# Attention beside a gated MLP on one core: a reordered opening, transposed sums for the last softmax reciprocals, and retuned scheduling constants

## The chip, the cores and the metric

The kernel runs on one core of one Trainium2 chip. The metric is the device time of one execution in microseconds, as the median of several runs. All runs compared here are fast (within 1.5% of the fastest run of the same kernel). The granted clock is the share of full speed that TensorE's clock had, as the profile gives it. Inside a trace, times count from the start of the span; the span is some 2 us shorter than the device time.

## The reference

```python
B, S, D, H, F = 1, 2048, 512, 32, 1792            # Dh = 16
def _A_ref(x, wqkv, wo):
    qkv = (x @ wqkv).reshape(B, S, 3, H, Dh).transpose(2, 0, 3, 1, 4)
    q, k, v = qkv[0], qkv[1], qkv[2]
    p = softmax(einsum("bhqd,bhkd->bhqk", q, k) * Dh ** -0.5)
    o = einsum("bhqk,bhkd->bhqd", p, v)
    return o.transpose(0, 2, 1, 3).reshape(B, S, D) @ wo
def _B_ref(x, W_gate, W_up, W_down):
    gate = x @ W_gate
    return (gate * (gate > 0) * (x @ W_up)) @ W_down
xn = _layernorm(A_x)                               # eps 1e-5
return A_x + _A_ref(xn, A_wqkv, A_wo) + _B_ref(xn, B_W_gate, B_W_up, B_W_down)
```

Softmax over 32 heads of 2048 x 2048 scores is 134 million exponentials. That is the load that everything else is arranged around.

## The kernel before

The program does not write its instructions in order. It describes each as an operation with an engine, a modelled duration, what it reads and writes, and a priority. A list scheduler then fixes one static order for each engine from these durations, before the kernel is built. Semaphores keep the result right whatever the true durations are; the order stays as it is.

```python
def op(self, eng, dur, fn, reads=(), writes=(), prio=0.0, ...)   # dur: modelled ns
...
key = (late, at if late else 0.0, o.prio - (self.KEEP if same else 0.0), o.idx)
```

Scores are made on TensorE; ScalarE evaluates most exponentials, in units of three and two PSUM banks in turn, into a ring of buffers in SBUF. A fifth of the groups (98 of 512) gets its exponential on VectorE, by bit manipulation. The exponentials are then multiplied with v on TensorE ("PV" from here on); a column of ones beside v gives the softmax sums. An eviction is a copy of a result out of PSUM into SBUF. For most head groups the sums are inverted on GpSimd by way of DRAM, far off the path. The last two groups can't wait for that. They spread each head's sum over 32 partitions with a matmul and invert the spread tile:

```python
def sums(e):                                            # last-but-one group
    for j in range(4):
        ins = e.matmul(ps_b[32*j:32*j+32, 1, :], ident32[:, 32*j+DH:32*j+DH+1].to_broadcast([128, 32]),
                       o_sb[:, to.slot, :], start=True, stop=True, tile_position=(0, 32*j))
    return ins
G.op("PE", 920, sums, ...)
G.op("DVE", 680, lambda e: e.reciprocal(rb[:, tr.slot, :], ps_b[:, 1, :]), ...)
G.op("DVE", 610, lambda e: e.tensor_tensor(oT_of(tn), rb[:, tr.slot, :], o_sb[:, to.slot, :], ALU.mult), ...)
```

The last group does the same in two halves of 256 columns. After it come the last output matmuls, the residual additions and four transfers out.

In the opening, row statistics of four row tiles go through VectorE; GpSimd adds eps and raises to -0.5, tile by tile; tiles are normalised, transposed, evicted, and the first q and k chains (128 columns of x each, as four 32-column matmuls side by side) lead to the first scores.

The softmax here doesn't subtract the row's maximum and nothing guards it: scores larger than these inputs give would overflow.

Of the kernel before, what the change touches and what calls it, by code (L numbers as in the profile page):

```python
# [6 lines left out]
FP32 = mybir.dt.float32  # L7
# [22 lines left out]
PV_LAG = 3.0  # L30
PV_MIN = 2
NWS = 3
# [3 lines left out]
D_GROUPS = 98  # L36
D_SKIP = 14
D_TAIL = 6
D_LEAD = 9.0
D_WAIT = 1.0  # L40

XT_ACT = ((1,), ())
K_ACT = (1, 2, 3)
FIN_PE = (1,)
PV_FREE = 1
N_MUL = 4
V_ACT = (0, 1, 2, 4)
N_POOL = ()
HX = 4
O_END = 70  # L50
O_LAST = 74
O_BEG = 20
EV = -12.0
PACE_L = 0.9

# [33 lines left out]
class Graph:  # L89
# [4 lines left out]
    SWITCH = 100.0  # L94
    SLIP = 60.0
    KEEP = 8.0
    RIDE = 20.0
    WINDOW = 3400.0
# [332 lines left out]
def bass_parallel_sum__mha_block__glu_gated_reglu__prompt_kernel(  # L431
# [16 lines left out]
    with ExitStack() as es:  # L448
# [33 lines left out]
        up_sb = sb("up_sb", [128, NUP, 512], FP32)  # L482
        rb = sb("rb", [128, 2, 512], FP32)
        rsum = sb("rsum", [128, 2, 16], FP32)
        rrec = sb("rrec", [128, 2, 16], FP32)
# [110 lines left out]
        t_x0 = [Tile() for _ in range(4)]  # L596
        t_xn0, t_pro = [], []

        def ln_block(b, pr):
# [11 lines left out]
            for i in range(4):  # L611
                m = 4 * b + i
                t_st, t_mv = Tile(), Tile()
                G.op("DVE", 640, lambda e, m=m: e.bn_stats(stats[:, m, :], xs(m)), reads=[t_xm[m]], writes=[t_st], prio=pr)
                G.op("DVE", 130, lambda e, m=m: e.bn_aggr(mv[:, m, :], stats[:, m, :]), reads=[t_st], writes=[t_mv], prio=pr - 0.1)
                t_mvs.w.append(G.ops[-1])
                if first:
                    inv(m, 1, t_mv, t_rs[i])
            if not first:
# [5 lines left out]
            for i in range(4):  # L625
# [26 lines left out]
                if first:  # L652
                    def ev(e, bank=bank, m=m):
                        src = bank()[:, 0:512].rearrange("p (dt c) -> p dt c", dt=DT)
                        return e.activation(xnT[:, :, 128 * m:128 * m + 128], src, ACTF.Copy)
                    if i != 2:
                        o = G.op("ACT", 560, ev, reads=[tp], writes=[Tile()], prio=pr + 0.1)
                    else:
                        def ev(e, bank=bank, m=m):
                            src = bank()[:, 0:512].rearrange("p (dt c) -> p dt c", dt=DT)  # L660
                            return e.tensor_copy(xnT[:, :, 128 * m:128 * m + 128], src)
                        o = G.op("DVE", 610, ev, reads=[tp], writes=[Tile()], prio=pr + 0.1)
                    o.deps = {w: True for w in o.deps if w is tp.w[-1]}
# [39 lines left out]
        def first_chain(tile, sub, W, tw, prio, c0, c1):  # L703

            for dt in range(DT):
                def fn(e, dt=dt):
                    ins = None
                    for j in range(4):
                        ins = e.matmul(bank_of(tile, sub)[32 * j:32 * j + 32, c0:c1], W[:, dt, 32 * j:32 * j + 32], xnT[:, dt, c0:c1],
                                       start=(dt == 0), stop=(dt == DT - 1), tile_position=(0, 32 * j))  # L710
                    return ins
                o = G.op("PE", 25 + 55 * (c1 - c0) // 128 if c1 - c0 < 512 else 225, fn, mode="col", reads=[tw] + t_x0[c0 // 128:c1 // 128], writes=[tile], prio=prio)
                if W is Wq:
                    o.order.update(d for d in o.deps if d.eng == "PE")
                    o.deps = {w: True for w in o.deps if w in tw.w or any(w in t.w for t in t_x0[c0 // 128:c1 // 128])}
                    o.order = {d for d in o.order if d.dur < 400}
# [7 lines left out]
        def proj_q(c4, gg, prio=0.0, tile=None, sub=0, eng="DVE", slots=None):  # L724
            t = tile or Tile("pq", P_b, [1])
            prio = slots[-1] if slots else prio
            if (c4, gg) == (0, 0):
                for c0 in range(0, 384, 128):
                    first_chain(t, sub, Wq, t_wq[0], prio, c0, c0 + 128)
                first_chain(t_pro[1], 0, Wq, t_wq[0], prio - 20, 384, 512)  # L730
            else:
# [3 lines left out]
            if eng == "ACT":  # L735
                for tt, sb, c0, c1, up in ((t, sub, 0, 384, 0.0), (t_pro[1], 0, 384, 512, -20.0)):
                    n = (c1 - c0) // 128
                    G.op("ACT", 190 + 105 * n, lambda e, tt=tt, sb=sb, c0=c0, c1=c1: e.activation(
                        qm[:, tq.slot, 0, c0:c1], bank_of(tt, sb)[:, c0:c1], ACTF.Copy, scale=hmask[:, 0:1]),
                        reads=[tt, t_mask0], writes=[tq] if n == 3 else [t_q4], prio=prio + up)  # L740
                    o = G.ops[-1]
                    if n == 1:
                        tq.w.append(o)
                        o.order.add(tq.w[0])
                    o = G.op("DVE", 100 + 130 * n, lambda e, tt=tt, sb=sb, c0=c0, c1=c1: e.tensor_scalar(
# [121 lines left out]
        G.op("POOL", 2500, lambda e: e.memset(v_aug[:, :, :, DH:VN], 1.0), writes=[t_vones], prio=-500, lock=True)  # L867
        for o in t_xn0:
            G.ops[-1].deps[o] = True
# [151 lines left out]
        t_half, t_fin = [Tile(), Tile()], [Tile(), Tile()]  # L1021

        def last_normalise(to, pr):
            def src(a=0, b=512):
                return o_sb[:, to.slot, a:b]

            tn, tr = Tile("oT", P_oT), Tile("rb", P_rb)
            tt = [Tile("ls", P_b, [2]), Tile("lb", P_sc, [1])]
            for h in range(2):
                def bank(h=h):  # L1030
                    return ps_b[:, 2, 256 * h:256 * h + 256] if h == 0 else ps_sc[:, 3, 256 * h:256 * h + 256]

                def sums(e, h=h, bank=bank):
                    ins = None
                    for j in range(4):
                        ins = e.matmul(bank()[32 * j:32 * j + 32, :], ident32[:, 32 * j + DH:32 * j + DH + 1].to_broadcast([128, 32]),
                                       src(256 * h, 256 * h + 256), start=True, stop=True, tile_position=(0, 32 * j))
                    return ins
                o = G.op("PE", 460, sums, mode="col", reads=[t_half[h], t_id32], writes=[tt[h]], prio=pr - 100, name="sum")
                o.opens = ("tail", [o]) if h == 0 else ()  # L1040
                t_rec = Tile()
                G.op("DVE", 400, lambda e, h=h, bank=bank: e.reciprocal(rb[:, tr.slot, 256 * h:256 * h + 256], bank()), reads=[tt[h]], writes=[t_rec] + ([tr] if h == 0 else []),
                     prio=pr - 900, name="rec")
                if h:
                    tr.w.append(G.ops[-1])
                    G.ops[-1].order.add(tr.w[0])
                t_fin[h].w.append(G.op("DVE", 330, lambda e, h=h: e.tensor_tensor(oT_of(tn)[:, 256 * h:256 * h + 256], rb[:, tr.slot, 256 * h:256 * h + 256], src(256 * h, 256 * h + 256), ALU.mult),
                     reads=[t_rec, t_half[h]], writes=[tn] if h == 0 else [], prio=pr - 900, lock=True))
                if h:
                    tn.w.append(G.ops[-1])  # L1050
                    G.ops[-1].order.add(tn.w[0])
            return tn

        def normalise(c4, gg, ee):
# [15 lines left out]
            if (c4, gg, ee) == (NB - 1, NGG - 1, 0):  # L1070
                tn, tr, ts, t_rec = Tile("oT", P_oT), Tile("rb", P_rb), Tile("ls", P_b, [1]), Tile()

                def sums(e):
                    ins = None
                    for j in range(4):
                        ins = e.matmul(ps_b[32 * j:32 * j + 32, 1, :], ident32[:, 32 * j + DH:32 * j + DH + 1].to_broadcast([128, 32]),
                                       o_sb[:, to.slot, :], start=True, stop=True, tile_position=(0, 32 * j))
                    return ins
                G.op("PE", 920, sums, mode="col", reads=[to, t_id32], writes=[ts], prio=pr - 20, name="sum")
                G.op("DVE", 680, lambda e: e.reciprocal(rb[:, tr.slot, :], ps_b[:, 1, :]), reads=[ts], writes=[tr], prio=pr - 900, name="rec")  # L1080
                G.op("DVE", 610, lambda e: e.tensor_tensor(oT_of(tn), rb[:, tr.slot, :], o_sb[:, to.slot, :], ALU.mult),
                     reads=[tr, to], writes=[tn], prio=pr - 900, lock=True)
                t_oT[(c4, NGG + ee)] = tn
                return
# [37 lines left out]
        def pv_group(key, kt, u):  # L1122
# [12 lines left out]
            for k in range(3 if on else 1):  # L1135
                def pv(e, k=k):
                    ins = None
                    for j in range(4):
# [3 lines left out]
                    return ins  # L1142
                G.op("PE", 225, pv, mode="col", reads=rd, writes=[pv_tile[key]], prio=u + PV_LAG - (200 if u > NU - 5 else 0), name="pv%d" % u,
                     after=u + PV_MIN)
# [98 lines left out]
        for i in range(4):  # L1243
# [8 lines left out]
            if i in FIN_PE:  # L1252
                for k in range(4):
                    G.op("PE", 225, lambda e, i=i, tz=tz, k=k: e.matmul(bank_of(tz)[:, 128 * k:128 * k + 128], ident32[:], resid(i)[:, 128 * k:128 * k + 128], start=(k == 0), stop=False),
                         mode="full", reads=[t_id32, t_res[m]], writes=[tz], prio=NU - 20 if i == 3 else NU + 2)
            for g, pr in ((2, NU - 10), (4, NU - 9), (5, NU + 10)):
# [70 lines left out]
```

## Time and profile before

| | before |
|---|---|
| median of the first three runs | 790.53 us (790.36 to 791.13) |
| start of the first exponential | 11.37 us |
| last exponential ends | 776.07 us |
| ScalarE's listed gaps between these | 4.75 us, one of 3.72 |
| from the last exponential's end to the end | 12.03 us |
| span of the profiled run | 788.1 us |

Read the table as a sum: first exponential, plus ScalarE's stream, plus the tail, is the span. The lines behind it are in the prediction.

### The profile page before, as it was taken

How to read it: one execution, taken by the hardware profiler on the slowest of the kernel's cores; microseconds unless marked ns; L12 is line 12 of the kernel's file. 1: busy time of each engine (PE TensorE's matmuls, PEld its weight loads, DVE VectorE, ACT ScalarE, POOL GpSimd, SP SyncE). 2: the span in 40 equal slices, each digit the busy share in tenths (PEclk: the TensorE clock that was granted, in tenths of full speed). 3: DMA queues.
4: the chain of work that ended last, by engine and by line, in shares of the span. 5: the costliest groups of instructions: out<-in, count | busy, mean ns of one | idle time of the engine just before them, and what ended most of it. 6: DMA issues, size and time to landing. Idle time of an engine off the chain costs nothing.

```text
span 788.1 us, 21088 instructions
## 1 busy us (share of the span) xinstructions
PE 756.7 (96%) x9270; PEld 225.2 (29%) x9270; DVE 740.0 (94%) x1065; ACT 763.3 (97%) x679; POOL 165.0 (21%) x178
## 2 busy tenths in 40 slices
PE   8999999999999999999999999999999999999986
PEld 4322222222222222222222223222222222223322
DVE  7689999999999899999999999999999899999994
ACT  6999999999999999999999999999999999999992
POOL 4112131221222113122122112212211212212200
PEclk9999999999999999999999999999999999999998
DMA  7312121212221122211221112221222112332000
GB/s 215 108 47 65 41 70 36 63 48 61 56 70 42 36 62 63 68 46 47 72 56 51 42 49 76 51 66 32 73 55 69 35 53 71 71 82 55 29 15 28
DMA packets 95756, 46.82 MB, mean 59 GB/s; under 512 B 69936, under 2 KB 91824, under 8 KB 95664
## 3 DMA queue, kind: packets, MB, share of 16 engines
q1 hardware_dynamic: 95664, 45.46, 21.3%
q8 instruction: 73, 1.20, 0.6%
q14 instruction: 19, 0.16, 0.1%
HBM read 36.70 MB, written 8.50 MB: 57 GB/s over the span
## 4 chain that ended last, share of the span: by engine, by line
DVE 46%; PE 26%; ACT 26%; issue 1%; DVEq 0%
ACT ring L1232 25%; DVE dring L1180 16%; PE ps_b L697 10%; DVE dring L1196 8%; PE ps_sc L1164 7%; DVE dring L1197 6%; PE ps_b L1140 5%; DVE dring L1192 4%; DVE dring L1194 4%; DVE up_sb L916 3%; DVE hT L920 2%; PE ps_b L1164 2%; DVE Wv L1068 1%; PE ps_b L863 1%; DVE xn_sb L958 1%
## 5 line engine op out<-in xcount | busy, mean ns | idle before, releaser
L1232 ACT ACTIVATE ring<-ps_sc 128x1536 bf16<-128x1536 f32 (+1 forms) x663 | 755.2, 1279 | 6.6 <-PE ps_sc L1164 4.9
L1180 DVE TENSOR_SCALAR dring<-ps_b 128x512 uint16<-128x512 f32 x392 | 269.5, 687 | 19.4 <-PE ps_b L1164 18.8
L1164 PE MATMUL ps_sc<-qm,kT 32*128 32x512 bf16 x1656 | 264.7, 385 | 6.6 <-ACT ring L1232 4.1
L1164 PE MATMUL ps_b<-qm,kT 32*128 32x512 bf16 x392 | 150.1, 383 | 8.8 <-DVE dring L1180 6.3
L1140 PE MATMUL ps_b<-ring,v_aug 128*17 128x512 bf16 x1656 | 152.1, 384 | 0.3 <-DVE Wv L1068 0.2
L1094 POOL TENSOR_TENSOR rrec<-rsum,minus 128x16 f32<-128x16 f32 x30 | 96.3, 3211 | 228.6 <-DMA rsum<-Wv 228.6
L1164 PEld LDWEIGHTS ps_sc<-qm,kT 32*128 32x128 bf16 x1656 | 63.4, 91 | 231.5 <-ACT ring L1232 202.3
L1197 DVE TENSOR_TENSOR dring<-dring 128x2048 bf16<-128x2048 bf16 x98 | 119.5, 1219 | 0.0
L1196 DVE TENSOR_TENSOR dring<-dring 128x2048 f16<-128x2048 bf16 x98 | 119.4, 1219 | 0.0
L1104 POOL TENSOR_TENSOR x_sb<-Wv,rb 128x128 bf16<-128x128 f32 x100 | 46.3, 465 | 285.3 <-DVE dring L1197 77.7
L1192 DVE TENSOR_SCALAR dring<-dring 128x2048 uint16<-128x2048 uint16 x98 | 67.9, 693 | 1.7
L697 PE MATMUL ps_b<-xnT,wus 128*32 128x512 bf16 x896 | 67.9, 384 | 1.1 <-DVE hT L920 0.6
L1194 DVE TENSOR_SCALAR dring<-dring 128x2048 uint16<-128x2048 uint16 x98 | 67.6, 689 | 0.0
L697 PE MATMUL ps_b<-xnT,wgs 128*32 128x512 bf16 x896 | 66.2, 383 | 1.3 <-DVE up_sb L916 1.0
L1140 PE MATMUL ps_b<-dring,vd 128*17 128x512 bf16 x784 | 65.5, 381 | 0.0
L697 PE MATMUL ps_b<-Wd,hT 128*32 128x512 bf16 x768 | 59.8, 383 | 0.1
L1140 PEld LDWEIGHTS ps_b<-ring,v_aug 128*17 128x17 bf16 x1656 | 38.5, 89 | 65.3 <-issue 46.7
L1164 PEld LDWEIGHTS ps_b<-qm,kT 32*128 32x128 bf16 x392 | 35.6, 91 | 66.0 <-DVE dring L1180 52.9
L1140 PE MATMUL ps_b<-dring,v_aug 128*17 128x512 bf16 x392 | 38.6, 384 | 1.5 <-DVE dring L1197 0.7
L1282 PE MATMUL ps_b<-zeros 128*17 128x512 bf16 x456 | 38.9, 382 | 0.0
L916 DVE COPY up_sb<-ps_b 128x512 f32<-128x512 f32 x56 | 38.4, 686 | 0.2 <-PE ps_b L697 0.2
L920 DVE SCALAR_TENSOR_TENSOR hT<-ps_b,up_sb 128x512 bf16<-128x512 f32 x48 | 32.9, 686 | 0.9 <-PE ps_b L697 0.9
(105 smaller groups left out, 363.3 us busy)
## 6 DMA issues: line engine op xcount, KB each, us to landing
rb<-rec_scr SPq DMA_DIRECT2D x30, 256.0 KB
wus<-in_B_W_up_dram SPq DMA_DIRECT2D x56, 128.0 KB, 3.5
wgs<-in_B_W_gate_dram SPq DMA_DIRECT2D x56, 128.0 KB, 2.3
qm<-q_scr SPq DMA_DIRECT2D x30, 128.0 KB
o_scr<-x_sb SPq DMA_DIRECT2D x25, 128.0 KB
q_scr<-qT SPq DMA_DIRECT2D x17, 128.0 KB
xr_sb<-in_A_x_dram SPq DMA_DIRECT2D x16, 128.0 KB, 2.5
out_dram<-xn_sb SPq DMA_DIRECT2D x16, 128.0 KB, 1.8
```

The source lines that it names most:

```text
L697: ins = e.matmul(bank_of(tile, sub)[32 * j:32 * j + 32, :], st[:, 32 * j:32 * j + 32], mv, start=(i == 0), stop=(i == n - 1), tile_positio ...
L916: G.op("DVE", 610, lambda e: e.tensor_copy(up_sb[:, tup.slot, :], bank_of(tu)), reads=[tu], writes=[tup], prio=slots[1] + EV)
L920: G.op("DVE", 610, lambda e: e.scalar_tensor_tensor(out=h_of(th), in0=bank_of(tg), scalar=0.0, in1=up_sb[:, tup.slot, :], op0=ALU.max, op1 ...
L1094: G.op("POOL", 3000, lambda e: e.tensor_tensor(rrec[:, par, :], rsum[:, par, :], minus[:, 0:1].to_broadcast([128, 16]), ALU.pow), reads=[t ...
L1140: ins = e.matmul(ps_b[32 * j:32 * j + VN, 0, :], v, src[j][1](k), start=(first and k == 0), stop=(last and (k == 2 or not on)), tile_posit ...
L1164: return e.matmul(bank, kT[32 * j:32 * j + 32, gg, 128 * kt:128 * kt + 128], qm[32 * j:32 * j + 32, t_q[(c4, gg)].slot, ee, :], start=True ...
L1180: o = G.op("DVE", 610, lambda e, j=j: e.tensor_scalar(dring[:, tr.slot, 0, 512 * j:512 * j + 512].bitcast(U16), ps_b[:, 2, :], 0.25 * LOG2 ...
L1192: G.op("DVE", 600, lambda e: e.tensor_scalar(b(2, U16), b(0, U16), 0x7F, 0x3F80, op0=ALU.bitwise_and, op1=ALU.bitwise_or), reads=[tr], wri ...
L1194: G.op("DVE", 600, lambda e: e.tensor_scalar(b(1, U16), b(0, U16), 0xFF80, N_MANT, op0=ALU.bitwise_and, op1=ALU.bitwise_or), reads=[tr], w ...
L1196: G.op("DVE", 1140, lambda e: e.tensor_tensor(b(2, FP16), b(2), b(2), ALU.mult), reads=[tm], writes=[tm], prio=u - 3, name="d4", lock=True)
L1197: G.op("DVE", 1140, lambda e: e.tensor_tensor(b(2), b(0), b(2, FP16), ALU.mult), reads=[tm, tr], writes=[tm], prio=u - 3, name="d5", lock= ...
L1232: return e.activation(ring[:, a:a + n, :], ps_sc[:, 3 * k0:3 * k0 + n, :], ACTF.Exp, scale=0.25)
```

## The change

The intent: a shorter path to the first exponential, short reciprocals at the end. Cut to its core:

```diff
-PV_MIN = 2            +PV_MIN = 1
-D_SKIP = 14           +D_SKIP = 12
-XT_ACT = ((1,), ())   +XT_ACT = ((1,), (1,))
-FIN_PE = (1,)         +FIN_PE = ()
                       +PV_LAST = 14
-O_END, O_LAST, O_BEG = 70, 74, 20     +74, 58, 24
-EV, PACE_L = -12.0, 0.9               +-940.0, 1.2
-SLIP, KEEP, RIDE = 60, 8, 20          +200, 6, 40
 # opening: eps on VectorE, pow of two tiles, full-width chains, a q quarter on VectorE
-                if first:
-                    inv(m, 1, t_mv, t_rs[i])
+                if first and i % 2:
+                    o = G.op("DVE", 130, lambda e, m=m: e.tensor_scalar(vare[:, m-1:m+1], mv[:, m-1:m+1, 1], EPS, None, op0=ALU.add), ...)
+                    G.op("POOL", 740, lambda e, m=m: e.tensor_tensor(rstd[:, m-1:m+1], vare[:, m-1:m+1], expo[:, 0:2], ALU.pow), ...)
-                    for j in range(4):
-                        ins = e.matmul(bank[32*j:32*j+32, c0:c1], W[:, dt, 32*j:32*j+32], xnT[:, dt, c0:c1], ..., tile_position=(0, 32*j))
+                    return e.matmul(bank[:, c0:c1], W[:, dt, 0:128], xnT[:, dt, c0:c1], ...)
 # closing: sums transposed, inverted as 128 x 4 per chunk of 128 columns, then spread
+        for c in range(c0, c1):
+            ins = e.matmul(bank_s(4*c, 4*c+4), src(128*c, 128*c+128), ident32[:, DH:128:32], ...)
+        G.op("DVE", 180, lambda e: e.reciprocal(rrec2[:, par, 4*c0:4*c1], bank_s(4*c0, 4*c1)), ...)
+        for c in range(c0, c1):
+            for j in range(4):
+                ins = e.matmul(bank_r(32*j, 128*c), rrec2[:, par, 4*c+j:4*c+j+1].to_broadcast([128, 32]), ident32[:], ..., tile_position=(0, 32*j))
... (order constraints and buffer names left out)
```

`XT_ACT` moves one more eviction of 128x1024 normalised values to ScalarE. `FIN_PE` says which of the last four row tiles get their residual by identity matmuls on TensorE and are copied out by ScalarE; the others are added on VectorE. Of the other constants, `PV_MIN` and `PV_LAST` say how early a PV may run and from where on it goes first, `O_*` and `PACE_L` place and pace the output rows, `EV` is the priority of evictions, `D_SKIP` keeps the first groups on ScalarE, and `SLIP`, `KEEP` and `RIDE` steer the list scheduler.

## The prediction

> **What bounds the kernel now.** I read the busy line of the page first, then the windows table stage by stage, then ScalarE's waits, then the timeline of the two ends.
>
> ```profile
> PE 756.7 (96%) x9270; PEld 225.2 (29%) x9270; DVE 740.0 (94%) x1065; ACT 763.3 (97%) x679; POOL 165.0 (21%) x178
> ...
> 48.00:400.00 352.00, 341.50 (x4088) 98.58 (x4084) 343.55 (x481) 351.44 (x310) 77.42 (x76) 1.00 0.21 56
> 400.00:739.00 339.00, 331.19 (x4058) 97.04 (x4055) 326.67 (x455) 338.10 (x298) 74.20 (x73) 1.00 0.22 58
> ```
>
> Three engines are nearly full, so the page alone doesn't say which one is the limit. The windows do (columns: stretch, length, busy us of PE, PE weight load, DVE, ACT, POOL, clock, DMA): between 48 and 739 us ScalarE is busy 689.5 of 691 us. It evaluates 663 exponentials (line 1232), and every one but the last is in one of two shapes that alternate. Nothing in the change alters their number, as the count of groups given to VectorE stays 98. So the span is: time to the first exponential (11.37), then ScalarE's stream up to its last one (about 776.1), then a tail (12.0). Only gaps in the stream, other work put on ScalarE, and the two ends can move the time. ScalarE's own waits say where the gaps are:
>
> ```profile
> ACT xn_sb L1274 <- PE ps_sc L1262: 6.9, 1, 6.9
> ACT xnT L655 <- PE ps_sc L646: 5.5, 2, 5.0
> ACT ring L1232 <- PE ps_sc L1164: 4.9, 3, 3.7
> ```
>
> The last row is the one in the stream: 4.9 us in three waits, one of them 3.7. The first is the tail, the second the opening. The timeline shows what the 3.7 is:
>
> ```profile
> 764.82 3.35 DVE L1080 RECIPROCAL rb<-ps_b 128x512 f32<-128x512 f32 x1
> ...
> 768.22 0.11 PEld L1262 LDWEIGHTS ps_b<-Wo,x_sb 128*32 128x32 bf16 x4 [2.94 <-DVE rb L1080]
> ...
> 770.71 5.36 ACT L1232 ACTIVATE ring<-ps_sc 128x1536 bf16<-128x1536 f32 x5 [3.72 <-PE ps_sc L1164]
> ```
>
> The reciprocal of the last-but-one head group takes 3.35 us, while the kernel's own schedule was built with 0.68 for it. The next matmul in TensorE's queue (line 1262) needs the bank that the reciprocal reads, so TensorE stands 2.65 us, the scores behind it come late, and ScalarE runs dry for 3.72 us. In the windows the granted clock of 768.2 to 770.7 is 0.50, so the backlog is then worked off slowly. The tail has the same thing twice:
>
> ```profile
> 777.19 0.76 DVE L1061 COPY Wv<-ps_b 128x256 f32<-128x256 f32 x2 [7.34 <-PE ps_b L1140]
> ...
> 778.62 1.76 DVE L1042 RECIPROCAL rb<-ps_b 128x256 f32<-128x256 f32 x1 [0.68 <-PE ps_b L1036]
> ...
> 780.30 1.69 DVE L1042 RECIPROCAL rb<-ps_sc 128x256 f32<-128x256 f32 x1
> 781.91 0.69 DVE L1047 TENSOR_TENSOR x_sb<-rb,Wv 128x256 bf16<-128x256 f32 x2
> ...
> 782.77 1.29 DVE L1271 TENSOR_TENSOR xn_sb<-ps_sc,xnT 128x512 bf16<-128x512 f32 x2 [0.18 <-PE ps_sc L1262]
> ...
> 783.98 0.68 DVE L1271 TENSOR_TENSOR xn_sb<-ps_b,xnT 128x512 bf16<-128x512 f32 x1
> ```
>
> Here nothing is left to hide behind: 3.37 us of reciprocals lie on the path that ends the program.
>
> **What the Trainium skill says.** "VectorE: DVE Perf Modes", section "First, the fixed hardware budget": reciprocal is an iterative divide with a repeat count of 8. The trace agrees in kind: from 256 to 512 columns it grows by 3352 - 1725 = 1627 ns, so 6.36 ns a column, against 686 ns for a whole copy of 512. "TensorE: Matmul & The Clock Gate", section "The mechanism": matmuls keep strict program order. The stall above agrees: scores for ScalarE wait behind a matmul that they don't depend on. The same page, section "What's actually happening": the array's clock is halved after an idle window of about 3.4 us and is full again after a busy one. The trace shows 0.50 after an idle of 2.65 us.
>
> **The change, part by part.**
>
> Middle reciprocal. The old form makes the sums already spread over 32 partitions each and inverts 128x512. The new form transposes: four matmuls with the fp32 data as weights give 128x16 sums, these are inverted, and 16 small column-tiled matmuls spread them. Reciprocal: 6.36 x 16 = 0.10 us plus the intercept 1725 - 256 x 6.36 = 0.10 us, so about 0.20 in place of 3.35. TensorE pays: an fp32 128x128 weight load and its matmul (line 1254) step by 0.42 us with a 128-column moving operand; the weight part is about 0.30, so four are 1.2 us. The spread moves 4 x 128 fp32 columns in four column tiles, as the old sums did with 512 columns (1.07 us), so again 1.07. TensorE goes from 1.07 to 2.3 us, which the lost 2.65 us of stall and the half clock pay for. What is gained is the gap on ScalarE, 3.7 us. As TensorE is busy 25.80 of 25.80 us in the stretch before, I leave 0.3 for a late score: **-3.4**.
>
> Tail. From the last PV matmul's end (777.14) to the last addition's end (784.66) it is now 7.52 us. New, counted from that point: first half evicted 0.45; its two sums 0.65 to 1.15; reciprocal of 8 columns, 0.15 and a handover, 1.4; the other half's sums lie ahead of the spread, so spread one ends at about 2.35 and two at 2.9; multiplications end 2.75 and 3.3; the final matmuls follow; then four additions on VectorE from 3.3, one per 0.62 us plus the last one's end: 5.85. Now three additions go to VectorE and one to ScalarE; the fourth costs 0.6, and is in this. 7.52 - 5.85 = **1.7** saved. The identity matmuls of row tile 1 (line 1254) go too: one pair, 0.42 us, lay ahead of the last PV matmul: **0.4** more. From the last addition to the end the output transfer remains, 3.4 us as now.
>
> Opening. Now the chain is: four row statistics, rsqrt on GpSimd one tile at a time, the last one ending at 7.67, normalise tile 3 (7.71), transpose (8.35), eviction on ScalarE 0.60, q chain 0.41, two q evictions one after the other on ScalarE, scores, first exponential.
>
> ```profile
> 7.71 0.41 DVE L628 TENSOR_SCALAR xn_sb<-x_sb,mv,rstd 128x512 bf16<-128x512 bf16 x1 [0.46 <-POOL rstd L609]
> ...
> 8.79 0.60 ACT L655 ACTIVATE xnT<-ps_sc 128x512 bf16<-128x512 bf16 x1 [0.43 <-PE ps_sc L646]
> ...
> 9.95 0.58 ACT L738 ACTIVATE qm<-ps_sc,hmask 128x384 bf16<-128x384 f32 x1 [0.57 <-PE ps_sc L709]
> 10.43 0.36 ACT L738 ACTIVATE qm<-ps_b,hmask 128x128 bf16<-128x128 f32 x1
> 11.37 2.37 ACT L1232 ACTIVATE ring<-ps_sc 128x1536 bf16<-128x1536 f32 x2 [0.58 <-PE ps_sc L1164]
> ```
>
> The pair of 1 costs 0.58 and of 4 costs 1.05 us, so pow of two is 0.74; eps moves from 0.22 on GpSimd to about 0.13 on VectorE, which delays the first normalise by two such. Tile 3 then starts where tile 2 ends, about 0.2 us sooner. Eviction of tile 3 on VectorE takes 0.42 (the record of tile 2) in place of 0.60: 0.2, and tile 2's goes to an idle ScalarE. The q chain drops from 16 narrow to 4 full matmuls: at most 0.2. The two q evictions run beside one another on two engines: 0.4. Sum **-1.0**, first exponential at about 10.4. Against it: a second eviction of 128x1024 goes from VectorE to ScalarE in the stream, where one took 0.92 us of the chain: **+0.9**. The row statistics of tiles 5 and up now wait for the q quarter, by about 0.7 us, which can starve block 1's keys; VectorE is freed of that eviction in exchange, so I count zero.
>
> Retuned constants (priority of evictions, pacing and position of output rows, when PV may run): ScalarE is already full in the body, so they have nothing to win there. They can only keep or lose: **0**.
>
> Sum: -3.4 - 1.7 - 0.4 - 1.0 + 0.9 = -5.6; with 790.5 before, **784.9 us**, 0.7% faster.
>
> **The rivals.**
> First, a new wait takes the stall's place: sums, reciprocal and spread are now three handovers between TensorE and VectorE, and TensorE's queue is strict. If the spread stands in the queue before the reciprocal could get through VectorE (a 1.22 us operation can be ahead of it), TensorE again stands about 1.2 us, and of the 3.4 only some 2 remain: 786.3. For it: TensorE is 100% busy in the last 25 us, so there is no slack. Against it: other bank-free work is there, and the operation's modelled duration (0.18) is now close to my estimate, where the old one was off by a factor of five.
> Second, the retuning breaks the body: VectorE is 97% busy between 48 and 739 us ((343.55 + 326.67) / 691), and moved evictions could make TensorE and then ScalarE late. Half a per cent of gaps would be 3.8 us and leave 788.7. For it: little slack. Against it: ScalarE's waits are only 6.6 us in all now, so the two-deep score buffer absorbs such things.
> Third, the opening is worth more: if the second eviction on ScalarE falls into an idle stretch that exists anyway, its 0.9 costs nothing: 784.0. With a tail a microsecond better than worked out, 783.
>
> **Range and chances.** The middle and tail rest on measured durations; together they can err by about 1.5 us, the opening by 1, the body by 2, mostly upward. Range 782.0 to 787.6. A 2% change would need 15.8 us, which is more than all gaps and the whole tail saving together: faster 0.01, same 0.98, slower 0.01.
>
> **What would show it right or wrong.** Right: reciprocals of 0.15 to 0.25 us; no ScalarE wait over 1 us near 765; no clock of 0.50 there; first exponential at 10.2 to 10.6; from the last PV's end to the last addition's end 5.9 us; ScalarE still 99.7% busy from 48 to 739. Wrong: a TensorE wait on the new reciprocal or spread of over 1 us, the last addition's time set by something other than VectorE's four in a row, or ScalarE gaps of more than 2 us in the body.

## The result, and the profile after

The changed kernel took 783.83 us (783.31 to 784.07, four runs) against 790.44 for the kernel before: ratio 0.9914, 95% interval 0.9897 to 0.9931. Ratios are the mean time of one kernel's fast runs over that of the other's in the same rounds, so not quite the ratio of the medians quoted. The predicted 784.9 was 1.1 us too high.

The page's busy line and two rows of the windows table, in the columns that the prediction explains:

```profile
PE 757.5 (97%) x9226; PEld 225.6 (29%) x9226; DVE 734.8 (94%) x1068; ACT 762.6 (98%) x678; POOL 165.5 (21%) x172
...
48.00:400.00 352.00, 343.93 (x4105) 98.85 (x4097) 344.48 (x485) 351.13 (x310) 78.81 (x77) 1.00 0.21 56
400.00:739.00 339.00, 332.79 (x4103) 96.91 (x4099) 325.13 (x452) 337.84 (x298) 75.03 (x71) 1.00 0.22 58
```

The body is as full as it was: ScalarE is busy 688.97 of 691 us, where it was 689.54. The gain is elsewhere. ScalarE's waits:

```profile
ACT xnT L664 <- PE ps_sc L655: 4.8, 1, 4.8
ACT ring L1245 <- PE ps_sc L1177: 1.4, 5, 0.6
```

The wait of 3.7 us is gone, and no wait in the stream is over 0.27 (the 0.6 of the second row comes before the first exponential). The wait of 6.9 us in the tail is gone because ScalarE has no work there any more. The timeline of the last-but-one head group (start, duration, engine, line, operation):

```profile
751.18 21.03 ACT L1245 ACTIVATE ring<-ps_sc 128x1536 bf16<-128x1536 f32 x19
...
756.63 1.06 PE L1035 MATMUL ps_b<-ident,Wv 128*128 128x4 f32 x8
...
757.96 0.25 DVE L1041 RECIPROCAL rrec<-ps_b 128x16 f32<-128x16 f32 x1
...
758.81 0.81 PEld L1047 LDWEIGHTS ps_b<-ident,rrec 128*32 128x32 f32 x32 [0.23 <-DVE dring L1193]
758.81 1.08 PE L1047 MATMUL ps_b<-ident,rrec 128*32 128x128 f32 x32
```

ScalarE runs through all of it without a break (first line). The reciprocal takes 0.25 us. The three handovers cost TensorE no wait worth the name: 0.23 us before the spread. The window from 768.2 to 770.7, which had a granted clock of 0.50, now has 1.00. The tail:

```profile
772.88 0.76 DVE L1082 COPY Wv<-ps_b 128x256 f32<-128x256 f32 x2 [5.89 <-PE ps_b L1153]
...
774.00 0.21 DVE L1041 RECIPROCAL rrec<-ps_b 128x8 f32<-128x8 f32 x1 [0.37 <-PE ps_b L1035]
...
774.45 0.21 DVE L1041 RECIPROCAL rrec<-ps_sc 128x8 f32<-128x8 f32 x1 [0.24 <-PE ps_sc L1035]
...
775.99 1.89 DVE L1284 TENSOR_TENSOR xn_sb<-ps_sc,xnT 128x512 bf16<-128x512 f32 x3
...
777.79 0.68 DVE L1284 TENSOR_TENSOR xn_sb<-ps_b,xnT 128x512 bf16<-128x512 f32 x1
```

From the last PV matmul's end (772.44 + 0.39 = 772.83) to the last addition's end (778.47) it is 5.64 us, where it was 7.52. And the opening:

```profile
8.65 0.39 DVE L670 COPY xnT<-ps_sc 128x512 bf16<-128x512 bf16 x1
...
9.30 0.58 ACT L744 ACTIVATE qm<-ps_sc,hmask 128x384 bf16<-128x384 f32 x1 [0.62 <-PE ps_sc L717]
9.53 0.35 DVE L745 TENSOR_SCALAR qm<-ps_b,hmask 128x128 bf16<-128x128 f32 x1 [0.30 <-PE ps_b L717]
```

The two q evictions now overlap, and the first exponential starts at 10.46. As a sum, all from the two profiled runs:

| | before | after | difference |
|---|---|---|---|
| first exponential | 11.37 | 10.46 | -0.91 |
| ScalarE's stream | 764.70 | 761.76 | -2.94 |
| tail | 12.03 | 9.28 | -2.75 |
| span | 788.1 | 781.5 | -6.6 |

Some 0.3 us of the first row is luck of that run: kernels with the old opening in the experiments below start their first exponential at 11.06 to 11.14.

### The profile page after: what moved, and what is told of

Same layout as the page of the kernel before. It is cut to its first block, busy times and chain, and to the rows that moved or that the text cites. A ratio compares the mean times of both kernels' runs of the same rounds, so it can differ in the third digit from the quotient of the medians.

```text
span 781.5 us, 20994 instructions
## 1 busy us (share of the span) xinstructions
PE 757.5 (97%) x9226; PEld 225.6 (29%) x9226; DVE 734.8 (94%) x1068; ACT 762.6 (98%) x678; POOL 165.5 (21%) x172
## 4 chain that ended last, share of the span: by engine, by line
DVE 52%; PE 35%; ACT 10%; DMA 1%; issue 1%; POOL 0%; DVEq 0%; SPq 0%
DVE dring L1193 17%; PE ps_b L707 13%; ACT ring L1245 10%; PE ps_sc L1177 9%; DVE dring L1209 8%; PE ps_b L1153 8%; DVE dring L1210 8%; DVE dring L1205 4%; DVE dring L1207 4%; DVE up_sb L923 3%; PE ps_b L1177 3%; DVE hT L927 3%; DVE Wv L1089 1%; PE ps_b L1295 1%; DVE stats L616 1%
## 5 line engine op out<-in xcount | busy, mean ns | idle before, releaser
L1153 PE MATMUL ps_b<-ring,v_aug 128*17 128x512 bf16 x1656 | 149.2, 382 | 2.2 <-DVE Wv L1089 1.2
L1107 POOL TENSOR_TENSOR rrec<-rsum,minus 128x16 f32<-128x16 f32 x30 | 100.2, 3341 | 229.1 <-DMA rsum<-Wv 229.1
L1153 PEld LDWEIGHTS ps_b<-ring,v_aug 128*17 128x17 bf16 x1656 | 36.9, 89 | 68.2 <-issue 50.1
```

The source lines that it names most:

```text
L1107: G.op("POOL", 3000, lambda e: e.tensor_tensor(rrec[:, par, :], rsum[:, par, :], minus[:, 0:1].to_broadcast([128, 16]), ALU.pow), reads=[t ...
L1153: ins = e.matmul(ps_b[32 * j:32 * j + VN, 0, :], v, src[j][1](k), start=(first and k == 0), stop=(last and (k == 2 or not on)), tile_posit ...
```

## The experiments

Twelve kernels were run, all correct. The columns "first", "stream", "gaps" and "tail" are of the profiled run; gaps are the waits that ScalarE's timeline lists inside the stream. The profiled run is one execution and can lie off the median: 785.20 us against 783.58 for after_narrow, 785.00 against 783.97 for after_fin3, 788.33 against 786.86 for after_old_open, 793.27 against 791.14 for after_old_tuning.

| run | median us | ratio to before | first | stream | gaps | tail |
|---|---|---|---|---|---|---|
| before | 790.44 | 1 | 11.37 | 764.70 | 4.75 | 12.03 |
| the whole change | 783.83 | 0.9914 | 10.46 | 761.76 | 2.00 | 9.28 |
| mid_only | 785.77 | 0.9945 | 11.08 | 761.11 | 1.51 | 11.71 |
| tail_only | 787.70 | 0.9966 | 11.06 | 766.13 | 6.36 | 9.11 |
| mid_tail | 784.16 | 0.9914 | 11.09 | 762.26 | 2.37 | 9.35 |
| true_dur | 786.20 | 0.9950 | 11.08 | 760.95 | 1.14 | 12.17 |
| open_only | 796.79 | 1.0080 | 10.34 | 772.82 | 13.01 | 11.84 |
| retune_only | 796.04 | 1.0071 | 11.14 | 772.63 | 10.82 | 11.83 |
| after_old_open | 786.86 | 0.9953 | 11.07 | 766.20 | 6.03 | 9.23 |
| after_old_tuning | 791.14 | 1.0013 | 10.48 | 771.68 | 10.67 | 9.34 |
| after_xt_dve | 791.00 | 0.9999 | 10.47 | 770.40 | 8.69 | 9.13 |
| after_placebo | 784.59 | 0.9926 | 10.42 | 762.89 | 3.41 | 9.19 |
| after_narrow | 783.58 | 0.9912 | 10.60 | 763.51 | 2.98 | 9.29 |
| after_fin3 | 783.97 | 0.9917 | 10.49 | 763.80 | 3.49 | 8.91 |

The 95% intervals of the ratios are about ±0.0012 to 0.0019, so some 1 to 1.5 us; a difference of two ratios is known to some 2 us. A ratio's difference times 790.5 gives microseconds; that is how the differences below are worked out.

**mid_only**: the last-but-one group's transposed sums put into the kernel before.

```diff
+ spread_sums(lambda a, b: o_sb[:, to.slot, a:b], 0, 4, 0, ..., to, ts, tr, pr + 80)
- sums / reciprocal of 128x512; the multiply now reads the spread reciprocals from PSUM; nothing else
```

> The kernel before with only the transposed sums for the last-but-one head group. Theory (the 3.35 us reciprocal stops TensorE's queue and starves ScalarE once): the 3.72 us gap on ScalarE goes, no granted clock of 0.50 near 768, and the time falls by 3.0 to 3.8 us, to about 787.0. Rival (the handovers sums, reciprocal, spread put a new wait of over 1 us on TensorE): it falls by under 2.2 us, and ScalarE has a wait of over 1 us near 760 to 770. Second rival (the body's retuning is needed to use it): under 1 us.

It gained 0.0055 x 790.5 = 4.3 us, with 3.0 to 3.8 expected; the interval, about 1.2 us either way, reaches that. The gap was gone, the granted clock from 768.2 to 770.7 was 1.00, and no wait in ScalarE's stream was over 0.6 us. Both rivals fall.

**tail_only**: the last group's transposed sums, and `FIN_PE = ()`, put into the kernel before.

```diff
-FIN_PE = (1,)
+FIN_PE = ()
+ spread_sums(src, 2*h, 2*h + 2, 1, ...) for each half h, in place of sums and reciprocal of 128x256
```

> The kernel before with the transposed sums only for the last head group, and all four last rows added on VectorE. Theory: from the last PV matmul's end to the last addition's end 7.5 us become 5.6 to 5.9, and the identity matmuls of about 0.4 us no longer precede the last PV matmul; the time falls by 2.0 to 2.8 us, to about 788.0. The 3.7 us gap on ScalarE stays. Rival (the fourth addition on VectorE and the extra TensorE steps eat the gain): under 1 us.

It gained 2.7 us, and from the last PV matmul's end to the last addition's end it was 5.65 us, both as expected. The tail in the profile fell from 12.03 to 9.11; a new gap of 1.32 us behind the old one of 3.71 took part of that back in the profiled run, where the granted clock stayed at 0.50 from 767.3 to 774.1. What the sums and `FIN_PE` are worth by themselves was not run.

**true_dur**: no instruction is another, only two modelled durations.

```diff
-G.op("DVE", 680, lambda e: e.reciprocal(rb[:, tr.slot, :], ps_b[:, 1, :]), ...)
+G.op("DVE", 3300, lambda e: e.reciprocal(rb[:, tr.slot, :], ps_b[:, 1, :]), ...)
-G.op("DVE", 400, ...reciprocal of each half...)
+G.op("DVE", 1700, ...)
```

> The kernel before, no instruction changed, but the schedule is built with 3.3 us for the 512-column reciprocal and 1.7 for the 256-column ones in place of 0.68 and 0.40. Theory A (the gap comes from TensorE's strict order behind a wrongly placed matmul, not from VectorE being occupied): with the true duration that matmul goes behind the reciprocal in the queue, ScalarE's 3.7 us gap goes or falls under 1 us, and the time falls by about 3 us although the 3.35 us reciprocal is still there. Theory B (VectorE's 3.35 us themselves are missing, so the short reciprocal is needed): a gap of over 2 us stays and the time falls by under 1.2 us.

It gained 4.0 us. The order of every queue but TensorE's is the same as before, and TensorE's differs in one place (the instruction order, with - for before and + for this one, cut):

```
 L1164 Matmult ps_sc<-qm,kT 128x512 x2
+L1140 Matmult ps_b<-ring,v_aug 17x512 x16
+L1164 Matmult ps_sc<-qm,kT 128x512 x3
+L1140 Matmult ps_b<-ring,v_aug 17x512 x4
+L1164 Matmult ps_sc<-qm,kT 128x512 x2
+L1282 Matmult ps_b<-zeros 17x512 x8
 L1262 Matmult ps_b<-Wo,x_sb 32x512 x4
-L1140 Matmult ps_b<-ring,v_aug 17x512 x12
...
```

Two units of scores and their PV matmuls now stand ahead of the matmul that needs the reciprocal's bank (line 1262), and blank matmuls (`zeros`), which the scheduler puts in where it models TensorE as too little busy, fill the rest. Its timeline shows that the reciprocal is as long as ever:

```profile
756.86 15.17 ACT L1232 ACTIVATE ring<-ps_sc 128x1024 bf16<-128x1024 f32 x14
...
764.81 3.35 DVE L1080 RECIPROCAL rb<-ps_b 128x512 f32<-128x512 f32 x1
...
768.22 0.40 PE L1262 MATMUL ps_b<-Wo,x_sb 128*32 128x512 bf16 x4 [0.16 <-DVE rb L1080]
```

TensorE waits 0.16 us where it waited 2.65, and ScalarE runs through. So theory A holds: in the middle, VectorE's 3.35 us were never the loss. The loss was a matmul put into a strict queue by a duration that was wrong by a factor of five. The short reciprocal removes the same gap and gains no clearly resolved time beyond that (ratios 0.9945 and 0.9950, intervals overlapping). The right duration in the middle together with the new tail was not run.

**open_only**: the opening put into the kernel before, without the second eviction on ScalarE.

```diff
+ eps on VectorE, pow of two tiles, eviction of tile 3 on VectorE, full-width first chains,
+ q quarter on VectorE, order=t_after for the statistics of tiles 5 and up
```

> The kernel before with only the opening changed (eps on VectorE, pow of two, full-width first chains, q quarter on VectorE, statistics of tiles 5 and up held back), without the second eviction of normalised tiles on ScalarE. Theory: first exponential at 10.4 to 10.6 in place of 11.37, and the time falls by as much, 0.7 to 1.0 us. Rival (held-back statistics starve the keys of block 1, and the gain is given back): first exponential as early, but new ScalarE waits between 12 and 35 us, and the time falls by under 0.4 us.

The first exponential came at 10.34 as expected, and yet the kernel was 6.3 us slower than before. The time sits in ScalarE's gaps, and most of it not in the opening at all:

```profile
257.01 40.83 ACT L1237 ACTIVATE ring<-ps_sc 128x1536 bf16<-128x1536 f32 x36 [1.73 <-PE ps_b L1145]
...
753.54 11.40 ACT L1237 ACTIVATE ring<-ps_sc 128x1536 bf16<-128x1536 f32 x10 [1.87 <-PE ps_b L1145]
767.26 5.97 ACT L1237 ACTIVATE ring<-ps_sc 128x1536 bf16<-128x1536 f32 x5 [2.32 <-PE ps_b L1145]
775.71 1.02 ACT L1237 ACTIVATE ring<-ps_sc 128x1024 bf16<-128x1024 f32 x1 [2.47 <-PE ps_sc L1169]
```

Line 1145 here is the PV matmul: ScalarE waits for a ring buffer that a late PV matmul still has to read. Line 1169 makes the scores. Neither the theory nor the rival had foreseen this. A change in the first 11 us has laid all queues anew up to the end. The rival had named starved keys between 12 and 35 us; those are there too (gaps of 0.65, 0.27 and 1.12 us), but they are the smaller part.

**retune_only**: only the constants put into the kernel before.

```diff
 PV_MIN 2 -> 1, D_SKIP 14 -> 12, O_END/O_LAST/O_BEG, EV, PACE_L, SLIP, KEEP, RIDE; PV first in the last 5 -> 14 units
```

> The kernel before with only those constants changed. Theory (the constants fit one queue layout; the body of before has no gap to fill): 790 to 795, the 3.7 us gap or one like it still there, some new gaps of 1 to 2 us. Rival (the constants themselves bring a gain): under 789.

It was 5.6 us slower than before, with gaps again (one of 1.79 us at 108 us, one of 2.38 at 771), and a little above the 790 to 795 that were stated. Alone, the constants harm.

**after_old_tuning**: the changed kernel with the old constants.

```diff
 the same list, taken back
```

> The changed kernel with the constants of before (PV_MIN, D_SKIP, positions and pacing of output rows, EV, SLIP, KEEP, RIDE, and the last 5 instead of 14 units of PV first); the opening, both sets of transposed sums and the second eviction on ScalarE stay. Theory (the opening re-lays all queues, and the constants were retuned to take the gaps out again): 786 to 791, with several ScalarE gaps of 1 to 2.5 us in the body, as with the opening alone. Rival (as predicted, the constants win and lose nothing): within 1 us of 783.8, and no ScalarE gap over 0.7 us.

It was 7.8 us slower than the changed kernel (1.0013 against 0.9914), and so no faster than the kernel before, although tail and first exponential keep their gains. Three of its gaps:

```profile
266.52 219.29 ACT L1244 ACTIVATE ring<-ps_sc 128x1024 bf16<-128x1024 f32 x193 [1.88 <-PE ps_b L1152]
487.61 2.53 ACT L1244 ACTIVATE ring<-ps_sc 128x1536 bf16<-128x1536 f32 x2 [1.79 <-PE ps_sc L1176]
491.49 1.45 ACT L1244 ACTIVATE ring<-ps_sc 128x1536 bf16<-128x1536 f32 x1 [1.35 <-PE ps_sc L1176]
```

**after_xt_dve**: the second eviction of normalised tiles back on VectorE.

```diff
-XT_ACT = ((1,), (1,))
+XT_ACT = ((1,), ())
```

> The changed kernel with the second 128x1024 eviction back on VectorE. As predicted (0.9 us of ScalarE's stream): 782.9 to 783.2. Rival (the eviction on ScalarE falls into a stretch where it would wait for keys anyhow, or moving it re-lays the queues): 783.8 or more, with ScalarE waits of 0.5 us or more between 18 and 35 us.

It was 6.7 us slower, where the prediction had it 0.9 us faster. One gap sits where the rival had looked for it:

```profile
34.23 0.60 ACT L788 ACTIVATE kT<-ps_b 128x512 bf16<-128x512 f32 x1 [2.67 <-PE ps_b L707]
```

ScalarE waits 2.67 us for a key chain. Two more, 1.35 and 1.13 us, lie at 573 and 597 us, where nothing of that eviction is near (more on these two below).

**after_placebo**: the modelled duration of an exponential, by 1 ns in 427.

```diff
-exp_ops[u] = G.op("ACT", 75 + 427 * n, ex, ...)
+exp_ops[u] = G.op("ACT", 75 + 426 * n, ex, ...)
```

> The changed kernel, only the modelled duration of one exponential changed by 1 ns a bank in 427: no instruction is another, but the list schedule may come out in another order. Theory (a schedule's luck is worth 1 us or more): over 785, with ScalarE gaps of over 0.7 us that the changed kernel has not. Rival (the schedule is stable): within 0.6 us of 783.8.

ScalarE's and GpSimd's order stayed, TensorE's and VectorE's came out another. The time rose by about 0.9 us (0.9926 against 0.9914), which the intervals don't quite resolve: between the two stated cases. So one arbitrary new layout cost this kernel about 1 us, if anything; the 6 to 8 us above are more than that, though a single placebo doesn't say how wide the spread of layouts is.

**mid_tail**: both transposed sums and `FIN_PE = ()` in the kernel before; opening, constants and evictions of before.

```diff
 the edits of mid_only and tail_only together
```

> The kernel before with the transposed sums for the last two head groups and all four last rows added on VectorE, and nothing else: opening and constants of before. Theory (the two reciprocals are the whole gain; opening and constants only cancel one another): the gains of the middle alone (4.7) and of the tail alone (2.8) add up, less up to 1 us for the tail's fill: 782.5 to 784.0, the same as the whole change. Rival (the opening and the retuned constants bring their own gain of 0.9 us or more): 784.6 or more.

Its ratio is 0.9914, the same as the whole change's. By the ratio that is 783.7 us, as the theory had it; the median of 784.16 lies between the two cases. The rest of the diff, opening, constants and second eviction, is worth 0 ± 1.7 us together (both intervals taken together).

**after_old_open**: the changed kernel with the opening of before.

```diff
 the edit of open_only, taken back; constants and second eviction on ScalarE kept
```

> The changed kernel with the opening of before, the retuned constants and the second eviction on ScalarE kept. Theory (the constants fit the new opening's layout only): 788 to 795, ScalarE gaps of 1 to 2.5 us in the body. Rival (the constants are good for any opening, and only the first exponential comes 0.7 later): 784.3 to 785.

It was 3.1 us slower than the changed kernel; 0.6 us of that is the later first exponential, and ScalarE's gaps are 4 us more, with 1.68 us at 118 and 1.24 at 594 us. The time lies between the two cases that were stated; the mechanism is that of the theory.

**after_narrow**: the first chains as four 32-column matmuls again, with the schedule built as for full width, so that every queue keeps its order.

```diff
-return e.matmul(bank[:, c0:c1], W[:, dt, 0:128], xnT[:, dt, c0:c1], ...)
+for j in range(4):
+    ins = e.matmul(bank[32*j:32*j+32, c0:c1], W[:, dt, 32*j:32*j+32], xnT[:, dt, c0:c1], ..., tile_position=(0, 32*j))
```

> The changed kernel with the first q and k chains emitted as four 32-column matmuls again, while the schedule is still built as for one full-width matmul, so the order of every queue is the same. It shows the full-width chains by themselves. Theory (20 fewer instructions per chain shorten only the last q chain, 0.41 to some 0.3 us): first exponential 0.0 to 0.2 us later, time within 0.4 us of the changed kernel's 783.8. Rival (the narrow loads hold up TensorE): over 784.5.

The time is the same (0.9912). A chain of four full-width matmuls takes 0.39 us in the changed kernel and the sixteen narrow ones take 0.41 (with their weight loads, 8 and 32 instructions: 24 fewer, not 20). With the order held, full width gains nothing that can be seen.

**after_fin3**: a try at a better version.

```diff
-FIN_PE = ()
+FIN_PE = (3,)
```

> A try at a better version: the changed kernel with the residual of the last row tile added by identity matmuls on TensorE (which have their place well before the end, where TensorE runs blank matmuls) and the result copied out by the idle ScalarE, so that VectorE has three additions in the tail. Theory (the four additions in a row on VectorE set the end): 0.5 to 0.7 us less, about 783.2. Rival (the schedule is laid anew, and its luck is worth more than 0.6 us): 784 or more, with gaps on ScalarE that the changed kernel has not.

The tail did shorten, from 9.28 to 8.91 us, but the new order has a gap of 1.32 us at 247 us, and the time is the same (0.9917). The profiled execution was the slowest of five, so the gap needn't be in the others. The tail is of interest all the same. Counted from the last PV matmul's end (774.34 + 0.39 = 774.73), the additions end after 5.06 us, 0.58 sooner than in the changed kernel, but the program's end comes after 8.47 us, only 0.20 sooner. The transfers out are issued by one queue:

```profile
778.55 0.60 ACT L1287 ACTIVATE xn_sb<-ps_b 128x512 bf16<-128x512 f32 x1 [4.26 <-PE ps_b L1275]
778.62 1.91 SPq L1289 DMA_DIRECT2D out_dram<-xn_sb x4
```

```profile
777.90 0.93 SPq L1289 DMA_DIRECT2D out_dram<-xn_sb  x2
```

The first fence is of this run, the second of the changed kernel. Seen one by one, the last three of the four issues here follow one another with 0.04 us between them and take 0.34, 0.43 and 0.45 us, until 780.53, which is 0.74 after the last addition; in the changed kernel they are spaced by the additions, take 0.33 to 0.35 each, and the last ends at 778.83, 0.36 after it. Additions that come faster than the queue issues gain little.

No version tried is clearly faster than the changed kernel. mid_tail, after_narrow and after_fin3 tie with it.

## Why the prediction was right or wrong

**The number was right**, and two of its parts, the middle and the tail, were right for the stated reason. That the rest added up to about nothing, as predicted, was luck.

The middle: predicted -3.4, alone it measured -4.3. The 0.3 left for a late score was not needed. The reciprocal was estimated at 0.20 us and took 0.25; the sums at 1.2 and took 1.06; the spread at 1.07 and took 1.08. The first rival, a new wait between the handovers, did not come: the longest wait of TensorE there was 0.23 us. The prediction said that the old reciprocal's modelled duration had put a matmul into the wrong place, and true_dur shows it. What the prediction did not draw from this is that the repair of that number alone would do: the short reciprocal is not what the middle needed.

The tail: predicted -1.7 and -0.4, and the profiled tail fell by 2.75. Its terms are 1.88 from the last PV's end to the last addition's end, 0.46 from the last exponential's end to the last PV's end (1.07 to 0.61), and 0.41 from the last addition to the end (3.44 to 3.03). The last was taken as unchanged, "3.4 us as now". It was mis-sized because before, the four issues ran back to back behind results that were ready close together:

```profile
783.49 1.95 SPq L1276 DMA_DIRECT2D out_dram<-xn_sb  x4
```

They ended at 785.44, 0.78 us after the last addition. In the changed kernel it is 0.36.

**The step that failed** is "Retuned constants ... they have nothing to win there. They can only keep or lose: **0**", and with it the terms for the opening (-1.0) and the second eviction (+0.9) as separate sums. The argument looked at the body of the kernel before, which has gaps of 0.59 and 0.44 us only. But the body that the new opening makes is another one, as the scheduler lays every queue anew. The opening alone costs 6.3 us in place of bringing 1.0. Without the constants the changed kernel loses 7.8, and without the second eviction on ScalarE 6.7 where the prediction had a gain of 0.9. These three terms were to add up to -0.1 and together measure 0 ± 1.7 (mid_tail against the whole change), so the total survived, though nothing in the argument says why losses of 6 to 8 us should cancel; one by one they are wrong in size, the second eviction also in sign, and the opening in sign when it comes alone (in the company of the constants it is worth 3.1 us, by after_old_open). What held is the purely local part: the first exponential came at 10.46 where 10.4 was predicted. Against the usual start of the old opening, 11.06 to 11.14, that is a gain of 0.6 us and not of 1.0; the term of "at most 0.2" for the q chain measured 0.02 (0.41 to 0.39).

The second rival, that the retuning breaks the body, came true for the constants alone (retune_only) and not for the change as a whole: ScalarE is still busy 99.7% between 48 and 739 us, as the prediction asked. Two readings of the prediction need a word. Of the "4.9 us in three waits" one, of 0.58, comes before the first exponential; in the stream the waits are 3.72, 0.59 and, from a row that the prediction doesn't show, 0.44. And the clock didn't fall when TensorE went on at 768.22, but at 767.92, still in the idle stretch, and was back at 1.00 from 771.33.

The releasers that the trace names for the gaps are late PV matmuls, late scores and, for the 2.67 us in after_xt_dve, a late key chain. For a part of the gaps the traces show more: the granted clock. In the body it falls to 0.50 for stretches of 3.41, 6.83 or 10.24 us. Two rows of after_xt_dve, before and in such a stretch (columns as above):

```profile
589.67:593.08 3.41, 2.50 (x29) 0.61 (x24) 3.38 (x6) 3.41 (x4) 0.00 (x0) 1.00 0.14 42
593.08:596.50 3.42, 3.42 (x31) 0.64 (x23) 2.67 (x4) 2.72 (x3) 1.26 (x1) 0.50 0.36 79
```

TensorE had been busy for 2.50 of 3.41 us, the clock fell, and ScalarE, full until then, was busy for 2.72 of 3.42 us; a 512-column matmul that takes 0.38 us at full clock took 0.61 at 0.50 (line 1262 of the kernel before). The gap at 573 us there, those from 491 to 496 in after_old_tuning, that at 594 in after_old_open and that at 476 in mid_tail end in such a stretch or just behind it; those at 257 in open_only, 118 in after_old_open and 267 in after_old_tuning don't. The changed kernel, mid_only, true_dur, after_placebo and after_fin3 show no such stretch before the last exponential. That the clock makes these gaps is read from the traces and was not tested by a run. Nor need a stretch be in every execution: those of one kernel differ in mean clock and time (before: 788.70 us at 0.998, 791.25 at 0.992).

Why a given order makes PV late, or lets TensorE's busy time sink, at a given place, and which of the constants matters, stays open.

## What to carry to other kernels

Where queues are static and strict, give the scheduler measured durations first: one wrong by a factor of five cost about 4 us here, and correcting it won that back without touching an instruction. Don't add up the worth of parts of a change when each part lays all queues anew; try them alone and left out, with a placebo edit to see what a mere new order is worth, and keep the parts that carry the gain (here two, of a much longer diff). A reciprocal should be taken before a value is spread, when it lies on the path that ends the program.

## What the Trainium skill lacked or had wrong

- "VectorE: DVE Perf Modes", section "First, the fixed hardware budget", says that reciprocal is iterated eight times, and gives no cost. Measured from PSUM in fp32: 3352 ns for 512 columns, 1757 and 1694 for 256, 249 for 16 and 208 for 8. A copy of 512 takes 686.
- "TensorE: Matmul & The Clock Gate", section "What's actually happening", puts the fall to half clock after an idle window of about 3.4 us. Here windows that were idle only in part were enough. In the kernel before the clock fell 2.34 us into an idle stretch, and TensorE was busy for 1.07 of the 3.41 us up to the fall; ahead of seven falls in the bodies of six other runs it was busy for 2.06 to 2.85 of 3.41 us by the records, whose matmul ends are modelled (the mean of the body before is 0.97). Where the busy share has to lie for a fall these runs don't settle.
- No page that was read for this has a cost on this chip for issuing several transfers in a row from one queue ("DMA: Bandwidth & Descriptors" would be its place): 0.33 to 0.35 us each when spaced, as in the changed kernel's tail, and 0.34, 0.59, 0.43 and 0.45 when four come at once, as before the change. In the tail it takes part in setting the end.
- None of the pages read warns that a static list schedule can turn a change at one end into gaps at the other: gaps of 1.7 to 2.5 us at 257 and from 754 to 776 us, after a change within the first 11 us.
